# Background weight combinations spread over batches 1 to 3 and stored from SyncE, and low halves of w_out formed by GpSimd, in a fused Nystrom attention and MLP kernel

## The chip, the cores and the metric

The kernel runs on one core of a Trainium2 chip. The metric is the time of one execution on the device in microseconds. Before the change it is 814.55 us, the median of 3 runs (814.32 to 814.81).

## The reference: what is computed

The input is q, k and v of 4 batches, 8 heads, 576 positions and 64 dimensions. Each head goes through a Nystrom attention with 32 landmarks:

```python
q_lm = q.reshape(B, H, m, S // m, D).mean(axis=3)      # m = 32, S = 576
A, Bm, C = sm(q, k_lm), sm(q_lm, k_lm), sm(q_lm, k)    # softmax of scaled products
Z = Bm.T / (norm1(Bm) * norminf(Bm) + 1e-06)
for _ in range(6):
    Z = 2 * Z - Z @ Bm @ Z
x = A @ Z @ C @ v                                      # 2304 tokens x 512
```

Two feed-forward blocks follow, each with weights of 512 x 2048 and 2048 x 512. The first has a leaky rectifier with a slope per channel, the second a gate:

```python
h = x @ w_in;  x = (max(h, 0) + alpha * min(h, 0)) @ w_out
h = x @ w_in2; out = (h * clip(h + 3, 0, 6) / 6) @ w_out2
```

The four weight matrices arrive as 64-bit floats, and the kernel forms 32-bit ones itself.

## The kernel before, in words

Every value that is multiplied at good precision is kept as two halves: ScalarE casts it to a rounded high half (`hi`), and VectorE subtracts that from the value to get the low half (`lo`). The helper `split` (lines 126 to 130) does both, and a product is then three matmuls (`passes`, line 132).

**Stage 1** is attention and the first feed-forward block. The main loop (line 1100) has 128 items, numbered `n`: 4 batches of 32 items, and in a batch two blocks of tokens by 16 tiles of 128 hidden channels. Item `n` issues the 6 matmuls `h` of its own tile (`first`, line 755) and, two items later, the 12 matmuls `acc` with `w_out` (`second`, line 784). Between them ScalarE and VectorE apply the rectifier and split the result: L774, L775, then L128 and L129 on `gs`. The attention of the next batch runs in pieces between the items, one piece per tick (`tick`, line 1097). In batch 0 the first block multiplies by the unsplit words of `w_out`, and at items 14 to 29 the 16 tiles of `w_out` are split by `w_out_split` (line 702) for all later use.

**The background work** of stage 1 prepares the second feed-forward block, which uses a product scheme of 7 multiplications instead of 8. Its weights are cut into 32 subs (16 of `w_in2`, 16 of `w_out2`), and for each sub `forms2` (line 844) goes through five steps, in five consecutive ticks:

- step 0: ScalarE turns the 64-bit words into two parts (L859, L862)
- step 1: VectorE joins the parts (L865), and GpSimd forms four sums or differences of 128x128 (L852)
- step 2: the first three of the seven forms are split into the tile `fa`, and `fa` is stored to DRAM
- step 3: the other four are split into `fb`
- step 4: `fb` is stored

A new sub begins every third tick (`GAP = 3`, `tick2`, line 891), and at that tick the raw words of the sub after it are also loaded (`land2`). 98 ticks are needed. The loop gives one per item from item 22 on, so that the last falls on item 119; `while ticks[0] < GAP * len(subs) + 2` (line 1153) would make up for missing ones. Work of a tick is held behind the rectifier of items `n - 2` and `n - 3`. The tiles `fa` and `fb` share few buffers (`home2`, line 838): two in turn for the first nine tiles, then three in turn, of which one is a slot of `w_out`'s pool. Tile number 9, which is `fb` of sub 4, and tile number 8, which is `fa` of sub 4, have the same buffer.

**Stage 2** is the second feed-forward block, in three blocks of tokens. Its weights are streamed from DRAM into six buffers `st` (`stream`, line 942), which lie where the pools of stage 1 lay. The first unit needs the first two of them.

**The order.** The instructions of TensorE and SyncE stand in the order of the program text (`manual_schedule`, line 1094). Those of ScalarE, VectorE and GpSimd are ordered by a planner, which simulates times and takes what is ready by priority. Every engine then works its own list in order, and an instruction that waits holds up those behind it. SyncE issues all loads of stage 1, and the loads of `stream` come right behind the last tick in its list.

Of the kernel before, what the change touches and what calls it, by code (L numbers as in the profile page):

```python
# [64 lines left out]
def kernel(  # L65
# [60 lines left out]
    def split(hi, lo, src, rest=nc.vector):  # L126
        return (
            nc.scalar.copy(hi, src),  # L128
            rest.tensor_tensor(out=lo, in0=src, in1=hi.bitcast(F32), op=ALU.subtract),  # L129
        )  # L130
# [571 lines left out]
    def w_out_split():  # L702
        for kk in range(NK):
            wout.append(wa.tile([P, 2, 512], F32R, tag=f"s{(kk + NK) % (NK + 1)}", name=f"wout{kk}"))
            split(wout[kk][:, 0], wout[kk][:, 1], words[kk])
            yield True

    wo_gen, wo_split = Background(w_out_tiles()), Background(w_out_split())
# [135 lines left out]
    def forms2(n_):  # L844

        z, i, j = subs[n_]
        raw = raw2[n_]
        high, low = raw[:, :, :, 1], raw[:, :, :, 0]
        x, y = low.bitcast(F32), high.bitcast(F32)

        def combine(o, p, q_, op):
            nc.gpsimd.tensor_tensor(out=y[:, o], in0=p, in1=q_, op=op)  # L852

        def stored(f, fs):
            to = w1_d[:, i, j, fs] if z == 0 else w2_d[:, fs, i, j]
            nc.gpsimd.dma_start(out=to, in_=f.bitcast(F32))  # L856

        if wide:
            nc.scalar.activation(  # L859
                out=high.bitcast(F32), in_=high.bitcast(F32), func=AF.Prelu, scale=2.0 ** -112, alpha=-(2.0 ** 32)  # L860
            )
            nc.scalar.activation(out=low, in_=low.bitcast(U32), func=AF.Copy, scale=0.9374 * 2.0 ** -29)  # L862
        yield True
        if wide:
            nc.vector.scalar_tensor_tensor(  # L865
                out=low, in0=high, scalar=3, in1=low, op0=ALU.logical_shift_left, op1=ALU.bitwise_or
            )
        if z == 0:
            combine(0, x[:, 1], x[:, 0], ALU.subtract)
            combine(2, x[:, 0], x[:, 3], ALU.add)  # L870
            combine(1, x[:, 3], y[:, 0], ALU.subtract)
            combine(3, x[:, 2], y[:, 1], ALU.subtract)
        else:
            combine(0, x[:, 0], x[:, 1], ALU.subtract)
            combine(1, x[:, 3], x[:, 0], ALU.subtract)
            combine(2, y[:, 1], x[:, 1], ALU.add)
            combine(3, y[:, 2], x[:, 2], ALU.subtract)
        yield True
        fa = home2().tile([P, 3, 2, P], F32R, tag=tags2[-1], name="fa")
        split(fa[:, :, 0], fa[:, :, 1], x[:, 1:4])  # L880
        stored(fa, slice(0, 3))
        yield True
        fb = home2().tile([P, 4, 2, P], F32R, tag=tags2[-1], name="fb")
        split(fb[:, :, 0], fb[:, :, 1], y)
        yield True
        stored(fb, slice(3, 7))
# [207 lines left out]
    with tc.manual_schedule(engines={mybir.EngineType.PE, mybir.EngineType.SP}):  # L1094
        pend = []

        def tick(n):
            bg.step(1)

        for n, (x, kk) in enumerate(items):  # L1100
            b, at_ = divmod(n, per)
            if b == 0 and at_ < NK:
                for i, (gen, upto) in enumerate(((wo_gen, min(at_ + 2, NK)), (w_gen, min(at_ + 11, NK + 5)))):
                    with behind(started if at_ < 3 else steps[at_ - 2] + steps[at_ - 3]):
                        gen.step(max(0, upto - emitted[i]))
                    emitted[i] = max(upto, emitted[i])
                if at_ % 4 == 3 and at_ // 4 + 1 < NC:
                    project(0, at_ // 4 + 1)
            if b == 0 and at_ >= NK - 2:
                upto = min(NK, at_ - NK + 3)  # L1110
                with behind(items[n - 1][0].last):
                    wo_split.step(upto - emitted[2])
                emitted[2] = upto
            if b == 0 and at_ in (NK + 4, NK + 6):
                c = NC // 2 + (at_ - NK - 4) // 2
                nc.gpsimd.dma_start(out=keep[:, c], in_=wins[c])
            if b == 0 and at_ == 6:
                bg.add(pinned(rest[0]))
            if b == 0 and at_ == 8 or b and at_ == 5:
                if b + 1 < B:  # L1120
                    bg.add(rush(attention(b + 1, two, 1), 300))
            if b + 1 < B and at_ in (28, 30):
                if at_ == 28:
                    bg.finish()
                project(b + 1, (at_ - 28) // 2)
                fetch(part(b + 1, 2 + (at_ - 28) // 2))
            if b and at_ in (1, 3):
                project(b, 2 + at_ // 2)
            if b == B - 1 and at_ == 4:
                stx.close()  # L1130
                yp = pool("yp", 1, side="right")
                load_y(0)
                y0 = Background(forms_y(0))
            pend.append((n, x, kk, x.first(kk)))
            if n < 3:
                warm((2, 3, 8)[n])
            tick(n)
            while pend and n >= pend[0][0] + (LOOK + 1 if pend[0][2] == 0 else LOOK):
                _, x0, kk0, gs = pend.pop(0)
                for _ in x0.second(kk0, gs):  # L1140
                    tick(n)
                tick(n)
            if n >= NK + 6:
                with behind(steps[n - 2] + steps[n - 3]):
                    tick2()
                    if b == B - 1 and at_ > 6 and at_ % 3 == 0:
                        y0.step(1)
        while pend:
            _, x0, kk0, gs = pend.pop(0)
            drain(x0.second(kk0, gs))  # L1150
        y0.finish()

        while ticks[0] < GAP * len(subs) + 2:
            tick2()

        sty.close()
        NST, NS = 6, 6
        tp = pool("tp", 1)
        stp = pool("st", NST)
        gp_ = pool("g", 1)  # L1160
        sp_ = pool("s", NS)
        g = gp_.tile([P, NK, TB], F32, name="g")
        shomes = [(sp_, "s") if x == "s" else (rp, x) for x in "r0 f0 s s r1 s s f1 s s r2".split()]
        shomes = [(sp_, "s") if x == "s" else (rp, x) for x in "r0 f0 s s r1 s s f1 s s r2".split()]
        ring, sums = [0], {}
        stream(NST)
        for i in range(NB):
            if i + 1 < NB:
                load_y(i + 1)
            for u in range(NU):  # L1170
                unit1(i, u)
            later = Background(forms_y(i + 1)) if i + 1 < NB else Background()
            for n_ in range(7):
                product2(i, n_)
                later.step(1)
            later.finish()
# [32 lines left out]
```

## Time and profile before

| What | Value |
|---|---|
| median of 3 runs | 814.55 us |
| the profiled execution's own time | 816.88 us |
| span of the profile | 815.1 us |
| TensorE busy | 792.8 us (97%) |
| VectorE busy | 594.5 us (73%) |
| ScalarE busy | 464.7 us (57%) |
| GpSimd busy | 185.6 us (23%) |
| DMA, mean over the span | 234 GB/s |

The profile shows one execution, with times in us from the start of its span. PE is TensorE's matmul, DVE is VectorE, ACT is ScalarE, POOL is GpSimd and SP is SyncE. L134 is line 134 of the kernel. The span runs from about 163 us on in batches 1 to 3, and stage 2 begins at about 454 us. TensorE's granted clock is at its full level in nearly all of the span.

### The profile page before, as it was taken

The page shows a single profiled execution, that of the slowest core. Times are in us where ns is not written, and L with a number is a line of the kernel's source. Part 1 is how long each engine was busy: PE and PEld are TensorE (multiplying, and loading weights), DVE is VectorE, ACT ScalarE, POOL GpSimd, SP SyncE. Part 2 cuts the span into 40 slices and gives each one's busy share as a digit, 9 for nine tenths or more (in the row PEclk, how much of TensorE's full clock was granted, in tenths as well). Part 3 has the DMA queues.
Part 4 walks back from the last instruction along what each step waited for, and adds up shares of the span by engine and source line. Part 5 has one row for each costly group of instructions (what it writes and reads, how often), then busy time and mean ns, then how long its engine had stood idle before and what let it go on. Part 6 is the DMA issues. An engine that isn't in the chain of part 4 may idle for free.

```text
span 815.1 us, 16385 instructions
## 1 busy us (share of the span) xinstructions
PE 792.8 (97%) x6146; PEld 739.4 (91%) x6146; DVE 594.5 (73%) x1215; ACT 464.7 (57%) x998; POOL 185.6 (23%) x275
## 2 busy tenths in 40 slices
PE   9788998999999999999999999999999999999997
PEld 6467787888988999988999999999999999999997
DVE  5778688768876778767795477994676994677962
ACT  4697556657665765666664455752455742555541
POOL 0000003244324433443660232000232000322000
PEclk9999999999999999999999999999999999999999
DMA  8998505587384973559655677777867677666751
GB/s 230 408 413 246 137 27 134 215 234 252 117 252 166 318 241 118 173 181 338 211 170 207 262 297 271 283 269 246 319 225 285 259 288 254 246 265 266 260 224 59
DMA packets 92559, 190.87 MB, mean 234 GB/s; under 512 B 39232, under 2 KB 66368, under 8 KB 85824
## 3 DMA queue, kind: packets, MB, share of 16 engines
q1 hardware_dynamic: 82944, 151.55, 53.4%
q0 software_dynamic: 9536, 38.28, 13.5%
q8 instruction: 48, 0.79, 0.4%
q14 instruction: 31, 0.25, 0.1%
HBM read 146.81 MB, written 42.99 MB: 233 GB/s over the span
## 4 chain that ended last, share of the span: by engine, by line
PE 85%; ACT 4%; DVE 4%; DMA 4%; issue 1%; SPq 1%; DVEq 0%; ACTq 0%
PE acc L134 20%; PE l L134 20%; PE qa L1038 15%; PE h L134 11%; PE qb L1038 7%; PE acc L793 2%; PE wp L683 2%; PE sa L433 2%; PE tp L276 1%; PE sc L347 1%; DMA raw<-in_moe_w_out_dram 1%; PE psr L517 1%; DMA raw<-in_moe_w_in_dram 1%; DMA yr<-y_d 1%; DMA w_d<-fa 1%
## 5 line engine op out<-in xcount | busy, mean ns | idle before, releaser
L134 PE MATMUL acc<-gs,wout 128*128 128x288 f32 (+1 forms) x1344 | 207.4, 300 | 0.0
L134 PEld LDWEIGHTS acc<-gs,wout 128*128 128x128 f32 x1344 | 186.1, 188 | 3.4 <-issue 1.5
L134 PE MATMUL l<-yf,st 128*128 128x384 f32 x1008 | 175.5, 335 | 0.7 <-DVE g L985 0.7
L134 PEld LDWEIGHTS l<-yf,st 128*128 128x128 f32 x1008 | 174.6, 188 | 1.0 <-DVE g L985 1.0
L1038 PE MATMUL qa<-st,s 128*128 128x256 f32 x1008 | 148.4, 283 | 0.0
L1038 PEld LDWEIGHTS qa<-st,s 128*128 128x128 f32 x1008 | 133.2, 192 | 0.0
L134 PE MATMUL h<-a,w 128*128 128x288 f32 (+2 forms) x768 | 129.4, 304 | 2.8 <-DVE gs L775 1.9
L128 ACT CAST s<-g 128x384 fp32r<-128x384 f32 x168 | 84.4, 512 | 80.5 <-PE qb L1038 54.2
L134 PEld LDWEIGHTS h<-a,w 128*128 128x128 f32 x768 | 108.4, 188 | 21.2 <-DVE gs L129 5.1
L129 DVE TENSOR_TENSOR s<-g,s 128x384 fp32r<-128x384 f32 x168 | 89.3, 560 | 20.4 <-ACT s L128 17.6
L852 POOL TENSOR_TENSOR raw<-raw 128x128 f32<-128x128 f32 x128 | 74.3, 592 | 76.0 <-DVE raw L865 41.2
L1038 PE MATMUL qb<-st,s 128*128 128x256 f32 x504 | 87.9, 283 | 0.0
L999 POOL TENSOR_TENSOR p<-p,p 128x384 f32<-128x384 f32 x24 | 26.3, 1095 | 237.9 <-ACT p L994 237.9
L774 ACT ACTIVATE t<-h 128x288 f32<-128x288 f32 (+2 forms) x120 | 49.5, 412 | 51.4 <-PE h L134 50.8
L775 DVE SCALAR_TENSOR_TENSOR t<-t,beta,h 128x288 f32<-128x288 f32 (+1 forms) x112 | 57.5, 513 | 28.2 <-ACT t L774 27.5
L1038 PEld LDWEIGHTS qb<-st,s 128*128 128x128 f32 x504 | 72.6, 192 | 0.0
L129 DVE TENSOR_TENSOR gs<-t,gs 128x288 fp32r<-128x288 f32 (+1 forms) x112 | 56.3, 503 | 18.3 <-ACT gs L128 17.9
L128 ACT CAST gs<-t 128x288 fp32r<-128x288 f32 (+1 forms) x112 | 49.0, 438 | 28.0 <-DVE t L775 26.4
L856 POOL DMA_DIRECT2D w_d<-fb x32 | 21.1, 661 | 77.0 <-DVE fb L129 47.6
L984 ACT ACTIVATE ta<-l,three 128x384 f32<-128x384 f32 x24 | 14.0, 583 | 38.5 <-PE l L134 38.5
L793 PE MATMUL acc<-gs,raw 128*128 128x256 f32 x128 | 31.8, 383 | 0.0
L990 ACT COPY p<-l 128x384 f32<-128x384 f32 x24 | 11.5, 479 | 34.5 <-PE l L134 34.5
(204 smaller groups left out, 1053.9 us busy)
## 6 DMA issues: line engine op xcount, KB each, us to landing
st<-w_d SPq DMA_DIRECT2D x48, 896.0 KB, 6.0
st<-w_d SPq DMA_DIRECT2D x42, 1024.0 KB, 5.5
w_d<-fb POOLq DMA_DIRECT2D x32, 512.0 KB, 4.2
w_d<-fa POOLq DMA_DIRECT2D x32, 384.0 KB, 3.2
raw<-in_moe_w_in_dram SPq DMA_DIRECT2D x16, 512.0 KB, 11.8
raw<-in_moe_w_out_dram SPq DMA_DIRECT2D x16, 512.0 KB, 11.5
raw<-in_moe_w_in_dram SPq DMA_DIRECT2D x64, 128.0 KB, 4.9
raw<-in_moe_w_out_dram SPq DMA_DIRECT2D x64, 128.0 KB, 4.8
```

Of the source, the lines that this page charges most:

```text
L128: nc.scalar.copy(hi, src),
L129: rest.tensor_tensor(out=lo, in0=src, in1=hi.bitcast(F32), op=ALU.subtract),
L134: nc.tensor.matmul(ps, lhsT=lhs(x), rhs=rhs(y), start=first and i == 0, stop=last and i == 2, **kw)
L433: nc.tensor.matmul(o[:, :, j], lhsT=qT[:, j, t * P:t * P + n], rhs=bdk[:, j], start=True, stop=True)
L683: nc.tensor.matmul(ps[g][js], lhsT=bd_t[b][gp, js], rhs=w[gp, j, cols], start=True, stop=True)
L774: nc.scalar.activation(out=t, in_=h, func=AF.Relu, scale=-1.0),
L775: nc.vector.scalar_tensor_tensor(out=gs[:, 0] if plain else t, in0=t, scalar=beta[:, kk:kk + 1], in1=h, op0=ALU.mult, op1=ALU.add),
L793: nc.tensor.matmul(acc, lhsT=words[kk][:, ms], rhs=gs[:, 0], start=at_ == 0, stop=at_ == NK - 1)
L852: nc.gpsimd.tensor_tensor(out=y[:, o], in0=p, in1=q_, op=op)
L856: nc.gpsimd.dma_start(out=to, in_=f.bitcast(F32))
L999: nc.gpsimd.tensor_tensor(out=p7, in0=p7, in1=p5, op=ALU.add)
L1038: nc.tensor.matmul(to[t], lhsT=s[:, y, t * P:(t + 1) * P], rhs=w[:, kp % 4, :, z], start=kp == 0 and m == 0 and t != 1, stop=kp == NU - 1 ...
```

## The change

Three things change. The low halves of `w_out` are formed by GpSimd in two pieces of 256 columns, while ScalarE still casts the high halves. The stores of `fa` and `fb` are issued by SyncE instead of GpSimd, and the store of `fa` moves to the beginning of the next step. The ticks run in every item from batch 1 on (items 32 to 127, 96 ticks), and the two that are left run behind the loop. A repeated line, which assigns the same value twice, is dropped.

```diff
@@ def w_out_split():
-            split(wout[kk][:, 0], wout[kk][:, 1], words[kk])
+            nc.scalar.copy(wout[kk][:, 0], words[kk])
+            for cs in (slice(0, 256), slice(256, 512)):
+                nc.gpsimd.tensor_tensor(
+                    out=wout[kk][:, 1, cs], in0=words[kk][:, cs], in1=wout[kk][:, 0, cs].bitcast(F32), op=ALU.subtract
+                )
             yield True
@@ def stored(f, fs):
-            nc.gpsimd.dma_start(out=to, in_=f.bitcast(F32))
+            nc.sync.dma_start(out=to, in_=f.bitcast(F32))
@@ forms2, step 2 and 3
         split(fa[:, :, 0], fa[:, :, 1], x[:, 1:4])
+        yield True
         stored(fa, slice(0, 3))
-        yield True
         fb = home2().tile([P, 4, 2, P], F32R, tag=tags2[-1], name="fb")
@@ main loop
-            if n >= NK + 6:
+            if b:
                 with behind(steps[n - 2] + steps[n - 3]):
                     tick2()
@@ stage 2
-        shomes = [(sp_, "s") if x == "s" else (rp, x) for x in "r0 f0 s s r1 s s f1 s s r2".split()]
         shomes = [(sp_, "s") if x == "s" else (rp, x) for x in "r0 f0 s s r1 s s f1 s s r2".split()]
```

## Rows read from the trace of the kernel before

**Rows 1.** The page, part 1: busy us, share, instructions.

```profile
PE 792.8 (97%) x6146; PEld 739.4 (91%) x6146; DVE 594.5 (73%) x1215; ACT 464.7 (57%) x998; POOL 185.6 (23%) x275
```

**Rows 2.** Windows: busy us and count by engine, clock, DMA share, GB/s.

```profile
100.00:150.00 50.00, 47.30 (x398) 42.84 (x398) 39.54 (x101) 30.89 (x76) 9.37 (x14) 1.00 0.27 77
150.00:200.00 50.00, 47.84 (x386) 42.47 (x385) 36.12 (x65) 32.38 (x71) 19.90 (x35) 1.00 0.83 262
...
400.00:450.00 50.00, 50.00 (x380) 50.00 (x380) 37.88 (x68) 29.50 (x65) 19.00 (x26) 1.00 0.53 185
```

**Rows 3.** TensorE's timeline, 100 to 200 us: start, us, work, [idle before, releaser].

```profile
133.46 0.69 PE L517 MATMUL psr<-nx 128*128 128x96 f32 x4 [0.81 <-ACT nx L530]
...
139.39 0.66 PE L517 MATMUL psr<-nx 128*128 128x96 f32 x4 [0.82 <-DVE nx L534]
...
142.24 0.34 PE L463 MATMUL atp<-ident,epc 64*128 64x64 f32 x2 [0.89 <-DVE a L129]
...
183.73 0.66 PE L276 MATMUL tp<-ident,rk 128*128 128x128 f32 x4 [1.50 <-ACT kT L277]
...
187.09 0.46 PE L276 MATMUL tp<-ident,rk 64*128 64x64 f32 x4 [0.67 <-ACT kT L277]
```

**Rows 4.** ScalarE's timeline ahead of the first of these gaps.

```profile
131.42 0.66 ACT L128 CAST fb<-raw 128x512 fp32r<-128x512 f32 x1
131.98 0.68 ACT L859 ACTIVATE raw<-raw 128x512 f32<-128x512 f32 x1
132.55 0.66 ACT L862 ACTIVATE raw<-raw 128x512 int32<-128x512 uint32 x1
133.10 0.51 ACT L530 ACTIVATE nx<-psr,cs 128x64 f32<-128x64 f32 x2
```

**Rows 5.** VectorE's timeline ahead of the next two gaps.

```profile
136.03 0.69 DVE L865 SCALAR_TENSOR_TENSOR raw<-raw 128x512 int32<-128x512 int32 x1
...
140.30 0.55 DVE L129 TENSOR_TENSOR fa<-raw,fa 128x384 fp32r<-128x384 f32 x1
```

**Rows 6.** Tile wout: duration ns min/median/max, first and last start.

```profile
L129 DVE TENSOR_TENSOR wout<-raw,wout x16: 673/686/693, 94.0 to 154.0; 128x512 fp32r<-128x512 f32 x16
```

**Rows 7.** Tiles raw and p: subtractions and sums on GpSimd.

```profile
L852 POOL TENSOR_TENSOR raw<-raw x128: 399/518/1320, 123.5 to 425.5; 128x128 f32<-128x128 f32 x128
...
L999 POOL TENSOR_TENSOR p<-p,p x24: 1007/1015/1342, 457.6 to 747.0; 128x384 f32<-128x384 f32 x24
```

**Rows 8.** Tile gs: the low half of an item's result on VectorE.

```profile
L129 DVE TENSOR_TENSOR gs<-t,gs x112: 437/459/823, 104.3 to 450.7; 128x288 fp32r<-128x288 f32 x96, 128x320 fp32r<-128x320 f32 x16
```

**Rows 9.** ScalarE's timeline, 160 to 200 us.

```profile
181.81 0.65 ACT L128 CAST fb<-raw 128x512 fp32r<-128x512 f32 x1 [3.67 <-DMA w_d<-fa]
```

**Rows 10.** SyncE's timeline, 130 to 200 us.

```profile
158.63 5.65 SPq L822 DMA_DIRECT2D raw<-in_moe_w_in_dram  x8
165.83 6.64 SPq L240 DMA_DIRECT2D rq<-in_q_dram  x5
```

**Rows 11.** Tile w_d: the 64 stores, us from issue to landing.

```profile
DMA to landing us min/median/max: 2.6/4.8/10.2
```

**Rows 12.** VectorE's timeline, 415 to 456 us.

```profile
420.01 0.69 DVE L865 SCALAR_TENSOR_TENSOR raw<-raw 128x512 int32<-128x512 int32 x1
...
426.73 0.69 DVE L129 TENSOR_TENSOR fb<-raw,fb 128x512 fp32r<-128x512 f32 x1
...
442.54 0.52 DVE L775 SCALAR_TENSOR_TENSOR t<-t,beta,h 128x288 f32<-128x288 f32 x1 [0.91 <-ACT t L774]
```

**Rows 13.** SyncE's timeline, 425 to 475 us.

```profile
436.46 18.46 SPq L947 DMA_DIRECT2D st<-w_d  x6
```

**Rows 14.** Line 947 from 440 to 443 us: two of these loads.

```profile
L947 SPq DMA_DIRECT2D st<-w_d x2: 422/424/425, 440.0 to 440.5; - x2
...
DMA to landing us min/median/max: 6.2/7.0/7.9
```

**Rows 15.** TensorE's timeline, 425 to 460 us.

```profile
453.71 6.58 PE L134 MATMUL l<-yf,st 128*128 128x384 f32 x37
```

## The prediction

> **What bounds the kernel now.** I read the page's busy times first: TensorE is busy for 792.8 of 815.1 us and no other engine is near it [rows 1]. All that can be had or lost is therefore TensorE's idle time, and the second view, the windows of 50 us, says where that lies. From 400 to 450 us, in batch 3, TensorE is busy all 50 us, and the 380 matmuls at 18 per item give 50 / (380 / 18) = 2.37 us per item, while VectorE has 37.9 us and ScalarE 29.5 us of work. From 100 to 150 us (batch 0) TensorE misses 2.7 us, and from 150 to 200 us 2.2 us [rows 2]. So the third view is TensorE's timeline there, which names five gaps. Three lie in batch 0: 0.81, 0.82 and 0.89 us, all at matmuls of the next batch's attention. Two lie in batch 1: 1.50 and 0.67 us at the transposes of k [rows 3]. The last view is what ScalarE, VectorE and SyncE did ahead of each gap, and around the passage to stage 2, since the change pushes work against that passage.
>
> **Batch 0: what is removed.** The change takes ten ticks out of items 22 to 31. Ahead of the first gap ScalarE worked off a cast of fb and two steps of raw, 0.57 + 0.57 + 0.55 = 1.68 us by the starts from 131.42 to 133.10, and only then the scaling of nx for which TensorE waited [rows 4]. All of the 1.68 us goes, which is more than the gap of 0.81 us. Ahead of the second and the third gap VectorE did a join of raw (0.69 us) and the low half of fa (0.55 us) [rows 5], besides low halves of wout, 16 of 0.69 us in all [rows 6], 11 us that go to GpSimd. I count all three gaps as gone: 0.81 + 0.82 + 0.89 = 2.5 us. Bounds: 2.5 us gained, or nothing if contention (below) holds the chain up as long; I take -2.5, since what goes is longer than each gap.
>
> **GpSimd's new work.** The trace has no 128x256 subtraction on GpSimd. From below it is a 128x128 one, 0.52 us, from above a 128x384 one, 1.02 us [rows 7]; I take the middle, an estimate of 0.77 us. Two per tile make 1.5 us, 16 tiles 25 us, at one tile per item, and an item of batch 0 is no shorter than 2.37 us. GpSimd has 9.4 us of work from 100 to 150 us [rows 2], most of it the sums and stores that leave. So it keeps up, and TensorE uses a tile of wout some items after its split: cost nothing, from cover of several items; without the cover a step would wait for the next cast of wout on ScalarE, under 1.5 us each.
> Its price lies on VectorE. The low half of gs takes 0.46 us in the median and 0.82 us at most, where a GpSimd sum runs beside it [rows 8]: up to 0.36 us for such an operation. With one such meeting per tile that is 16 x 0.36 = 6 us against the 11 us taken off, so VectorE is still relieved. The Trainium skill (SBUF — State Buffer, SBUF: two separate sides) states the harder rule that speaks against this part: a VectorE operation with two SBUF inputs and a GpSimd operation that reads SBUF exclude each other for a whole instruction. By that rule VectorE could lose the 25 us that GpSimd works, more than the 11 us it saves; the worst row shows half an instruction lost, so I give it a small chance as a rival.
>
> **Batch 1: a gap that is moved.** The cast of fb of sub 4 waited 3.67 us on ScalarE for the store of fa, which has the same buffer, to land [rows 9], and the copies of the transposes behind it came late: the gaps of 1.50 and 0.67 us. The buffers' order is kept, so this wait comes ten items later, when the next attention is past its transposes, with the store on SyncE's queue. A store landed in 2.6 to 10.2 us, 4.8 in the median [rows 11]. TensorE works two items ahead, 4.7 us; the four operations on an item's result take some 2 us of that (two of them 0.52 and 0.46 us [rows 8, 12]), so a result may be about 2.7 us late before TensorE runs dry. A landing of 2.6 us leaves no gap: 2.2 us gained. One of 4.8 us leaves 4.8 - 2.7 = 2.1 us: nothing gained. I take the middle, -1.0; a landing of 10.2 us would lose 5 us, and is put to the far end of the range.
>
> **Batch 1: the first sub.** Before, the words of sub 0 were loaded long before their tick. Now their loads stand behind the last fetch in SyncE's list, where the row of 158.63 us stands today: 8 issues in 5.65 us, so sub 0's four end near 161.5 us, and with about 6 us to land, as the loads of [rows 14], they are there near 167 us, while ScalarE may want them from 161 us on [rows 10]. Bounds: nothing, or 5.5 us of waiting less the 2.7 us, 2.8 us; I take +0.3, near the lower end, since the planner expects a load's delay as well. The load of q (issued from 165.83 us) now stands behind the stores of sub 0, which wait for VectorE, and slips by about four items, 9 us. It ended its issues at 172.5 us and is used by transposes behind those of 187 us [rows 3, 10]: hidden, with a few us of cover left, each us beyond it a us lost.
>
> **SyncE's queue in the steady part.** 64 stores add 64 issues of about 0.4 to 0.7 us to SyncE (by the loads of [rows 10, 14]), about 1 us of every 7.1 us that a sub takes. Behind a waiting store stand the next raw loads. They had to wait for the same split already, as it frees their buffer: 0, with 0 to +1 us as bounds. GpSimd is freed of its issues; nobody waits for it there.
>
> **The passage to stage 2: what is added.** The list of SyncE ends stage 1 with the stores of fa and fb of sub 31, then come the loads of st. Before, fb's tick fell on item 118 and its low half began at 426.73 us [rows 12]; the first load of st went out at 436.46 us, two others at 440.0 and 440.5 us [rows 13, 14], all landed well ahead of stage 2's first matmul at 453.71 us [rows 15]. Now the ticks of sub 31 lie ten items later, 23.7 us, and the loads are behind the store of fb. When is fb split? Its join waits for the rectifier of item 124, which ends at 442.54 + 0.52 = 443.1 us. Four sums on GpSimd of 0.52 us, the cast and the subtraction of 0.69 us each follow: 443.1 + 0.7 + 2.1 + 0.7 + 0.7 = 447.3 us at the earliest. In the trace the way from the join's start to the end of fb is 427.4 - 420.0 = 7.4 us [rows 12], which gives 450.5 us. I take the middle, D = 449 us. The wait and issue of the store take 0.5 us and the issue of the first load 0.4 us. The load issued next lands 6.2 us after its issue when another is just ahead of it [rows 14]. The store's own half megabyte is in front: 0 to 1.2 us, since a load of st, 896 KB by the code, adds 0.5 + 7.9 - 6.2 = 2.2 us to the one before it [rows 14] and fb has 512 KB; I take 0.6. The second buffer is then full at 449 + 0.9 + 6.2 + 0.6 = 456.7 us. TensorE wants it half a microsecond after 453.7 us, at 454.2: it waits 2.5 us. Bounds: D = 447.3 without the store ahead gives 0.2 us, D = 450.5 with 1.2 us gives 4.6 us. Batch 3 itself costs nothing: it ran without gaps with ticks and VectorE has 12 us free in 50 [rows 2].
>
> **The sum.** -2.5 - 1.0 + 0.3 + 0 + 2.5 = -0.7 us on the profiled execution's 816.88 us (its span is 815.1 us, the rest lies around it). That execution is 2.3 us above the median of the runs; the difference is carried over to the median: 814.55 - 0.7 = 813.9 us. What a measurement can tell from no change is 0.2%, 1.6 us: faster is below 812.9, slower above 816.2.
>
> **Rivals.**
> *The loads of st come late.* If the planner puts the last cast of fb behind the copies of the last sums (after 453 us), D is about 455 us, TensorE waits 456.7 + 6 - 454.2 = 8.5 us, and the time is near 820; behind the rectifier of item 127 (D = 451.5) it is 816.4. It decides from D = 451.3 on. For it: those two ticks have no item to hold them and stand last in the text. Against: their inputs are ready before, and ScalarE has 40% free. Between the two 818, chance 0.20.
> *The loads come in time.* D near 447.5 and the batch 1 gaps gone entirely: -2.5 - 2.2 + 0.3 + 0.4 = -4.0, 810.6; chance 0.20. For it: the ten items of batch 3 are lightly loaded. Against: fa's own store must land first as well.
> *The gaps only move.* The wait for the store of fa of sub 4 leaves its 2.2 us (no gain) and the late words of sub 0 cost 2.8 us: -2.5 + 0 + 2.8 + 2.5 = +2.8, 817.3 at worst; with half of the words' price 816; chance 0.10. For it: the two waits stand in the code. Against: the planner sees both.
> *Contention in batch 0.* VectorE loses as much as it saves, the 2.5 us stay: 813.9 + 2.5 = 816.4; chance 0.08. For it: the worst meeting of [rows 8]; against: the median of the same row. The Trainium skill's rule above would do this.
> *The forecast,* 813.9, has 0.42; alone it spans 812.0 to 816.0.
>
> **How the numbers follow.** Faster by over 0.2%: all of the second rival, 0.20, and 0.13 of the forecast: 0.33. Slower: 0.18 of the first, 0.04 of the third, 0.04 of the fourth and 0.01 of the forecast: 0.27. Within: 0.40. The range is 810.6 to 818: below it lies little, above it the far end of the first rival.
>
> **What would show it.** Right: no gap at psr and atp from 130 to 143 us; the gaps of 183 and 187 us gone or at a wait for fb near item 47; the first load of st at 449 to 451 us behind the store of fb, and a TensorE gap of 2 to 3 us ahead of the first l, released by a load. Wrong: gaps in batches 2 and 3, VectorE operations lengthened all through batch 0, no gap ahead of stage 2, or one above 5 us.

## The result, and the profile after

The changed kernel is slower: 824.42 us in the median of 4 runs (823.34 to 828.21), against 814.68 us (4 runs, 814.32 to 815.7) for the kernel before. The ratio is 1.0126, with a 95% interval of 1.0092 to 1.016. The forecast was 813.9 us, in a range up to 818. The profiled execution of the changed kernel took 823.34 us, with a span of 821.3 us, 6.2 us longer than the 815.1 us of before.

Part 1 of the page of the changed kernel, which answers to [rows 1] (busy us, share, instructions):

```profile
PE 794.5 (97%) x6146; PEld 739.1 (90%) x6146; DVE 588.5 (72%) x1199; ACT 465.4 (57%) x998; POOL 172.7 (21%) x243
```

TensorE's work is the same 6146 matmuls; VectorE has 16 operations and 6 us less, GpSimd 32 instructions less (64 stores gone, 32 subtractions come). TensorE's idle time grows from 22.3 us to 26.8 (span less busy time): most of the 6.2 us went there, and the windows say where. Windows of the changed kernel, columns as in [rows 2]:

```profile
100.00:150.00 50.00, 49.65 (x422) 44.30 (x421) 31.94 (x83) 26.63 (x70) 21.62 (x28) 1.00 0.15 36
150.00:200.00 50.00, 49.69 (x391) 44.11 (x390) 33.69 (x60) 31.30 (x69) 12.36 (x22) 1.00 0.74 229
200.00:250.00 50.00, 47.94 (x441) 44.73 (x439) 38.67 (x104) 30.04 (x80) 13.35 (x22) 1.00 0.60 181
300.00:350.00 50.00, 47.67 (x439) 42.75 (x437) 39.88 (x103) 29.34 (x78) 12.94 (x22) 1.00 0.51 169
400.00:450.00 50.00, 49.12 (x370) 48.66 (x369) 43.01 (x75) 36.02 (x77) 23.01 (x31) 1.00 0.61 195
450.00:500.00 50.00, 47.53 (x286) 46.88 (x285) 31.24 (x55) 24.26 (x45) 12.29 (x13) 1.00 0.87 336
```

From 100 to 200 us TensorE now misses 0.7 us, where it missed 4.9 [rows 2]: the part that the change was to mend is mended. But 200 to 250, 300 to 350 and 450 to 500 us miss 2.1 to 2.5 us each (before: 0.9, 0.5 and 0), and batch 3 (400 to 450 us), which ran without a gap, misses 0.9. The gaps of over 0.7 us by name, from TensorE's timeline of the changed kernel (columns as in [rows 3]):

```profile
203.12 0.74 PE L347 MATMUL sc<-kT,qlm 64*32 64x320 f32 x8 [1.53 <-ACT epc L373]
...
274.62 1.68 PE L683 MATMUL wp<-win,bd 64*32 64x512 f32 x16 [1.15 <-DVE w L129]
327.51 0.30 PE L480 MATMUL ctp<-ident,epc 128*64 128x128 f32 x1 [0.97 <-ACT ct L477]
344.07 0.34 PE L463 MATMUL atp<-ident,epc 64*128 64x64 f32 x2 [1.17 <-DVE a L129]
...
426.67 1.72 PE L134 MATMUL acc<-gs,wout 128*128 128x288 f32 x11 [0.78 <-DVE gs L129]
459.72 16.42 PE L134 MATMUL l<-yf,st 128*128 128x384 f32 x93 [1.41 <-DMA st<-w_d]
477.19 4.08 PE L134 MATMUL l<-yf,st 128*128 128x384 f32 x22 [1.05 <-DVE h L1013]
```

The gaps of [rows 3] are gone; these are new. None is long, and busy time hides how they add up, so a second measure helps. Both kernels have the same 6146 matmuls in the same order, so each can be set against itself: its start in the changed kernel less its start before. The delay is -2.33 us at the atp of 142.24 us [rows 3], -3.82 at the tp of 187.09, -1.63 at the wp that follows at 276 us, +0.06 at the ctp of 327 us, +1.25 at atp (343), +3.75 at acc (423), +3.86 at the first l [rows 15], and +6.2 at the end. So 3.8 us were won by 187 us, as forecast or better; 7.6 us were lost between 187 and 423 us, where nothing was expected; and the passage to stage 2, from its first l on, cost 2.35 us.

In the same way the start is read for every experiment below; "lost in batches 1 to 3" is the delay at 423 us less that at 187 us, "passage" what comes after 423 us. They are from one profiled execution each, and the ratios from all runs, 4 to 12 of each changed kernel against 4, 17 or 21 of the kernel before that were taken with them. The last tick's item follows from the item of the first.

The column "at 187 us" has to be read with care. At 120 us, before any edit has moved TensorE, the delay is already 0.9 to 1.3 us in e1, e4, e5, e6, e9 and e11 and 0.5 us in e7, and at most 0.3 us in the others: in these executions TensorE's granted clock was low for a while near 41 us (e1 had 0.66 from 40 to 50 us, the kernel before 1.00). From 120 to 187 us alone, e1 gains 2.5 us, e5 2.5, e11 1.5, and the changed kernel 4.0. What is lost behind 187 us isn't touched by this; the delay at the end is.

| Kernel | first tick | stores | ratio [95%] | at 187 us | lost in batches 1 to 3 | passage | end |
|---|---|---|---|---|---|---|---|
| changed | 32 | SyncE | 1.0126 [1.0092, 1.016] | -3.8 | 7.6 | 2.5 | +6.2 |
| e1_low | 22 | GpSimd | 0.9985 [0.9976, 0.9994] | -1.3 | -0.3 | -0.8 | -2.4 |
| e2_store | 22 | SyncE | 1.0098 [1.0083, 1.0114] | +3.6 | 3.5 | 0.5 | +7.6 |
| e3_shift | 32 | GpSimd | 1.0117 [1.0103, 1.0131] | -4.3 | 5.6 | 6.9 | +8.2 |
| e4_shift_low | 32 | GpSimd | 1.0138 [1.012, 1.0156] | -2.7 | 4.6 | 8.9 | +10.7 |
| e5_start31 | 31 | GpSimd | 1.0029 [1.0018, 1.004] | -1.4 | 0.2 | 2.1 | +0.9 |
| e6_start23 | 23 | GpSimd | 1.0039 [1.0026, 1.0053] | -2.6 | 5.3 | -0.5 | +2.1 |
| e7_end | 32 | GpSimd | 1.0109 [1.0091, 1.0126] | -3.9 | 4.5 | 7.5 | +8.1 |
| e8_store_early | 22 | SyncE, early | 1.0042 [1.0026, 1.0058] | -1.3 | 3.2 | -0.6 | +1.3 |
| e9_low28 | 28 | GpSimd | 1.0004 [0.9995, 1.0014] | -1.6 | 1.3 | -0.6 | -0.9 |
| e10_low25 | 25 | GpSimd | 0.9986 [0.9976, 0.9996] | -3.7 | 0.1 | 0.5 | -3.1 |
| e11_full31 | 31 | SyncE | 1.0079 [1.0066, 1.0092] | -0.6 | 4.4 | 1.6 | +5.4 |
| e12_early28 | 28 | SyncE, early | 1.0048 [1.0034, 1.0061] | -2.7 | 6.0 | -0.5 | +2.8 |

The low halves on GpSimd are in e1, e4, e9, e10, e11, e12 and in the changed kernel.

### The profile page after: what moved, and what is told of

It reads as the page before. It is cut to its first block, busy times and chain, and to the rows that moved or that the text cites. A ratio compares the mean times of both kernels' runs of the same rounds, so it can differ in the third digit from the quotient of the medians.

```text
span 821.3 us, 16439 instructions
## 1 busy us (share of the span) xinstructions
PE 794.5 (97%) x6146; PEld 739.1 (90%) x6146; DVE 588.5 (72%) x1199; ACT 465.4 (57%) x998; POOL 172.7 (21%) x243
## 4 chain that ended last, share of the span: by engine, by line
PE 75%; DMA 9%; DVE 6%; ACT 5%; issue 2%; SPq 2%; POOL 1%; DVEq 0%; ACTq 0%; POOLq 0%
PE l L134 20%; PE qa L1042 15%; PE acc L134 14%; PE h L134 8%; PE qb L1042 7%; DMA raw<-in_moe_w_out_dram 4%; PE acc L797 2%; DMA st<-w_d 2%; DMA raw<-in_moe_w_in_dram 2%; DMA w_d<-fa 2%; PE sa L433 2%; PE wp L683 2%; PE tp L276 1%; SPq L826 1%; PE sc L347 1%
## 5 line engine op out<-in xcount | busy, mean ns | idle before, releaser
L856 POOL TENSOR_TENSOR raw<-raw 128x128 f32<-128x128 f32 x128 | 79.8, 639 | 189.8 <-DVE raw L869 126.1
L129 DVE TENSOR_TENSOR gs<-t,gs 128x288 fp32r<-128x288 f32 (+1 forms) x112 | 60.9, 544 | 22.5 <-ACT gs L128 22.1
L707 POOL TENSOR_TENSOR wout<-raw,wout 128x256 fp32r<-128x256 f32 x32 | 24.6, 789 | 41.9 <-ACT wout L705 28.9
## 6 DMA issues: line engine op xcount, KB each, us to landing
raw<-in_moe_w_in_dram SPq DMA_DIRECT2D x16, 512.0 KB, 11.2
```

The source lines that it names most:

```text
L707: nc.gpsimd.tensor_tensor(out=wout[kk][:, 1, cs], in0=words[kk][:, cs], in1=wout[kk][:, 0, cs].bitcast(F32), op=ALU.subtract)
```

## Experiments

### Each part by itself: e1 to e4

**The low halves alone.**

```diff
@@ w_out_split
-            split(wout[kk][:, 0], wout[kk][:, 1], words[kk])
+            nc.scalar.copy(wout[kk][:, 0], words[kk])
+            for cs in (slice(0, 256), slice(256, 512)):
+                nc.gpsimd.tensor_tensor(
+                    out=wout[kk][:, 1, cs], in0=words[kk][:, cs], in1=wout[kk][:, 0, cs].bitcast(F32), op=ALU.subtract
+                )
```

> Only the low halves of w_out go to GpSimd; ticks from item 22 and stores by GpSimd as before. Queue theory (the 7.6 us lost in batches 1 to 3 come from the stores standing in SyncE's list) and position theory (they come from the ten items' shift, which sets the background work against other pieces of attention and fills the end of batch 3) both expect no loss in batches 1 to 3 here: 812 to 815 us, with up to 2 us of the three batch 0 gaps regained. The contention rival expects 815 to 818.

Measured: 814.36 us, ratio 0.9985 [0.9976, 0.9994], a gain of 0.15%, in the range that both theories gave. The new subtractions on GpSimd in the changed kernel, then VectorE's low halves of gs from 93 to 153 us, beside which they run, in the kernel before and in e1:

```profile
L707 POOL TENSOR_TENSOR wout<-raw,wout x32: 737/747/1011, 94.2 to 152.2; 128x256 fp32r<-128x256 f32 x32
L129 DVE TENSOR_TENSOR gs<-t,gs x12: 473/484/810, 104.3 to 150.5; 128x320 fp32r<-128x320 f32 x12
L129 DVE TENSOR_TENSOR gs<-t,gs x12: 483/690/1028, 105.3 to 149.7; 128x320 fp32r<-128x320 f32 x12
```

The median of all 112 in the span of the changed kernel is 459 ns, as before [rows 8], but most of them lie where no subtraction runs. In the stretch with subtractions the median rises from 484 to 690 ns (618 in the changed kernel, 1061 at most): about 0.2 us for nearly every one of 12, some 2.5 us against the 11 us taken off VectorE. TensorE loses nothing by it. This part isn't where the time went.

**The stores alone**, with the first tick at item 22 as before. As in the change, the store of fa also moves a step later.

```diff
@@ stored
-            nc.gpsimd.dma_start(out=to, in_=f.bitcast(F32))
+            nc.sync.dma_start(out=to, in_=f.bitcast(F32))
@@ forms2, step 2 and 3
-        stored(fa, slice(0, 3))
         yield True
+        stored(fa, slice(0, 3))
```

> Only the stores move to SyncE (with the store of fa one step later); ticks from item 22. Queue theory: gaps in batches 1 to 3 as in the changed kernel, 818 to 822 us, and raw loads and stores issued later than before. Position theory: 814 to 816 us, with the gaps of 183 and 187 us still there.

Measured: 823.15 us, 1.0098 [1.0083, 1.0114], a little above the range of the queue theory. The stores by themselves cost nearly as much as the whole change. Of the first 3.6 us, 2.0 are lost at an acc and a wp of batch 1 (165 and 172 us), which wait 0.64 and 0.45 us for VectorE, and the rest at the transposes of k; TensorE, ScalarE and the windows of e2 there:

```profile
186.49 1.11 PE L276 MATMUL tp<-ident,rk 128*128 128x128 f32 x4 [2.27 <-ACT kT L277]
```

```profile
185.31 0.65 ACT L128 CAST fb<-raw 128x512 fp32r<-128x512 f32 x1 [2.82 <-DMA w_d<-fa]
```

```profile
180.00:185.00 5.00, 4.22 (x34) 3.98 (x32) 2.28 (x5) 1.40 (x4) 2.42 (x4) 1.00 0.68 239
185.00:190.00 5.00, 3.51 (x16) 3.50 (x17) 2.92 (x4) 4.15 (x9) 0.00 (x0) 0.66 0.26 105
```

It is the wait of [rows 9], for the store of fa of sub 4 to land, ended 3.5 us later in the span. Here that store went out 3.5 us after its split, where it was 1.1 us before; SyncE's list and the step by which it is later both enter. Behind the wait stands the copy kT, and TensorE's gap is 2.27 us where it was 1.50 [rows 3]. After the gap the granted clock is 0.66 in the next 5 us, a mean of time at the full level (2.4 GHz) and at the lower one (1.2): the gap is paid for again in slow matmuls.

**The later ticks alone.**

```diff
@@ main loop
-            if n >= NK + 6:
+            if b:
```

> Only the ticks move to items 32 to 127; stores by GpSimd. Queue theory: 810 to 814 us, since batch 0 and the two gaps in batch 1 are regained (4 us) and only the passage to stage 2 costs 1 to 3 us. Position theory: 818 to 822 us, with gaps in batches 1 to 3 at the same kinds of places as in the changed kernel.

Measured: 824.84 us, 1.0117 [1.0103, 1.0131], above the ranges of both theories. It wins 4.3 us by 187 us, loses 5.6 in batches 1 to 3 and 6.9 at the passage. The new gaps of batch 2 are those of the changed kernel, at ctp and atp, though SyncE issues no store here. At the passage, e3's TensorE, then SyncE, then windows:

```profile
457.73 0.80 PE L134 MATMUL l<-yf,st 128*128 128x384 f32 x3 [2.03 <-DMA st<-w_d]
460.51 4.85 PE L134 MATMUL l<-yf,st 128*128 128x384 f32 x14 [1.98 <-DMA st<-w_d]
```

```profile
452.83 3.71 SPq L947 DMA_DIRECT2D st<-w_d  x6
```

```profile
455.00:460.00 5.00, 1.51 (x9) 0.95 (x7) 0.87 (x2) 0.40 (x1) 1.43 (x2) 0.90 0.99 374
460.00:465.00 5.00, 4.49 (x14) 4.49 (x15) 0.00 (x0) 0.96 (x2) 0.00 (x0) 0.50 1.02 411
```

The loads of st go out at 452.83 us instead of 436 to 440 us [rows 13, 14], and TensorE waits 2.03 and 1.98 us for them; then the granted clock is 0.50, the lower level, for 5 us in which only 14 matmuls run. So the passage is late by the shift of the ticks alone, whoever issues the stores.

**The low halves and the later ticks**, both edits above, without the stores.

```diff
@@ w_out_split
-            split(wout[kk][:, 0], wout[kk][:, 1], words[kk])
+            nc.scalar.copy(wout[kk][:, 0], words[kk])
...
@@ main loop
-            if n >= NK + 6:
+            if b:
```

> Everything of the change but the queue: ticks in items 32 to 127 and low halves on GpSimd, stores by GpSimd. Queue theory: 810 to 814 us. Position theory: 819 to 824 us, near the changed kernel's 824.

Measured: 826.82 us, 1.0138 [1.012, 1.0156]: above both ranges and no better than e3, with the same two waits at l (1.98 and 2.03 us). The costs of e2 and e3, 1.0% and 1.2%, aren't additive, since the whole change comes to 1.26%. The changed kernel is e4 with the stores on SyncE, and isn't slower than e4: it loses 3.0 us more in batches 1 to 3 and 6.4 us less at the passage. What is lost ahead of the passage makes TensorE come later to loads that land no sooner, so it waits less for them.

### Why the later ticks lose time in batches 2 and 3: e5 and e6

A sub begins every third tick and the attention's pieces keep their items. A first tick at item 32 instead of 22 moves the background by ten items, which three doesn't divide: other steps now stand ahead of the same piece of attention. ScalarE ahead of the ctp of 327 us, in the changed kernel, and the like stretch of the kernel before:

```profile
324.88 0.41 ACT L778 ACTIVATE t<-h 128x288 f32<-128x288 f32 x1 [0.74 <-PE h L134]
325.19 0.67 ACT L128 CAST fb<-raw 128x512 fp32r<-128x512 f32 x1
325.75 0.69 ACT L863 ACTIVATE raw<-raw 128x512 f32<-128x512 f32 x1
326.32 0.66 ACT L866 ACTIVATE raw<-raw 128x512 int32<-128x512 uint32 x1
326.87 1.07 ACT L477 COPY ct<-ctp 128x512 f32<-128x512 f32 x2
```

```profile
323.37 0.65 ACT L128 CAST fb<-raw 128x512 fp32r<-128x512 f32 x1
323.92 0.68 ACT L859 ACTIVATE raw<-raw 128x512 f32<-128x512 f32 x1
324.49 0.67 ACT L862 ACTIVATE raw<-raw 128x512 int32<-128x512 uint32 x1
...
325.96 0.41 ACT L774 ACTIVATE t<-h 128x288 f32<-128x288 f32 x1 [0.17 <-PE h L134]
326.37 1.08 ACT L477 COPY ct<-ctp 128x512 f32<-128x512 f32 x2
```

Step 3 of a sub (the cast of fb) and step 0 of the next (two operations on raw) fall on one tick, 1.68 us of ScalarE by the starts. Before, this tick came an item ahead of the copy of ct; now it stands between a rectifier and the copy, and TensorE waits 0.97 us. If that is the cause, a start at 31 (nine items later) must lose nothing in these batches, and a start at 23 (one later) as much as 32.

```diff
@@ main loop, e5
-            if n >= NK + 6:
+            if n >= NK + 15:
```

> Ticks from item 31 on, stores and low halves as before: one item earlier than the shift alone, so that in batches 1 and 2 the three-item rhythm of the background work stands against the pieces of attention as it stood before (22 and 31 leave the same remainder by 3). Rhythm theory (the shift alone lost its 6 us in batches 1 to 3 because the casts and unpackings fell just ahead of the copies of ctp and atp in batch 2): no gap at ctp and atp in batch 2, delay against before at 380 us of -4 to -2 us; the passage to stage 2 still costs 1 to 6 us; 814 to 820 us. Lateness theory (it is the later and denser place, whatever the rhythm): gaps as with the shift alone, delay at 380 us of -1.5 to 0 us, 822 to 825 us.

```diff
@@ main loop, e6
-            if n >= NK + 6:
+            if n >= NK + 7:
```

> Ticks from item 23 on, stores and low halves as before: one item later than before, ten ticks still in batch 0, the rhythm that of the shift by ten items. Rhythm theory: gaps at ctp and atp in batch 2 (near 325 and 342 us) as with the shift alone, some 2 to 4 us lost there; 816 to 820 us. Lateness theory: no such gaps, 814 to 816 us.

Measured: e5 818.05 us, 1.0029 [1.0018, 1.004]; e6 819.32 us, 1.0039 [1.0026, 1.0053]. Both times and the gaps came as the rhythm theory has them, but e5's delay at 380 us didn't: -1.15 us, where -4 to -2 was expected (the 1.1 us that stand at 120 us included). TensorE of e5 from 300 to 350 us (only the lines with a wait for another engine), then of e6:

```profile
331.20 0.90 PE L492 MATMUL pu<-rv,ct 128*32 128x64 f32 x40 [0.35 <-ACT nx L497]
...
340.21 0.66 PE L463 MATMUL atp<-ident,epc 128*128 128x128 f32 x4 [0.19 <-DVE a L129]
```

```profile
326.06 0.30 PE L480 MATMUL ctp<-ident,epc 128*64 128x128 f32 x1 [0.97 <-ACT ct L477]
326.55 0.30 PE L480 MATMUL ctp<-ident,epc 128*64 128x128 f32 x1 [0.19 <-ACT ct L477]
...
342.69 0.34 PE L463 MATMUL atp<-ident,epc 64*128 64x64 f32 x2 [1.17 <-DVE a L129]
```

One item of shift brings the gaps of the changed kernel, 0.97 and 1.17 us at the same matmuls, and 5.3 us of loss in batches 1 to 3; nine items bring 0.2 us. Half of the 5.3 us lies at these two matmuls; of the rest, 2.3 us lie in batch 3, at an h (389 us of before) and around 420 us, in e3 as in e6 and not in e5. What stands ahead of those is open. Over all kernels whose stores stay on GpSimd, first ticks at 22, 25, 28 and 31 lose -0.3 to 1.3 us there, and 23 and 32 lose 4.5 to 5.6. The remainder by three decides, not the amount of the shift. What e5 still loses is the passage: 1.31 us of wait at l, 2.1 us in all, nearly as much as the 2.5 us that it gains from 120 to 187 us.

### The passage: e7

If only the shared buffer of the last fa and fb holds the loads of st back, these tiles kept out of the slot of w_out's pool should free them. The ticks are those of e3.

```diff
@@ home2
-        spare = i > 8 and i % 3 == 2
-        tags2.append(f"s{NK - 1}" if spare else f"f{i % 3 % 2 if i > 8 else i % 2}")
+        ring3 = 8 < i < 60
+        spare = ring3 and i % 3 == 2
+        tags2.append(f"s{NK - 1}" if spare else f"f{i % 3 % 2 if ring3 else i % 2}")
```

> The shift alone (ticks in items 32 to 127, stores by GpSimd), with the last two subs' tiles fa and fb kept out of the slot of w_out's pool, so that the first load of stage 2 doesn't wait for the last store of fa. Passage theory (with the shift alone, that store's landing at 452.7 us set the first load's issue at 452.8 us, TensorE stood 2.0 and 2.0 us and then ran at the lower clock level from 460 to 465 us): the loads go out near 441 us, no gap and no lower clock at the start of stage 2, 6 us less than the shift alone, 816 to 819 us. Rival (the stage's start is late for another reason, such as the loads' own time): 822 to 825 us.

Measured: 824.9 us, 1.0109 [1.0091, 1.0126]; the expectation failed. The loads did go out early, but the stores of the last subs then came late. SyncE, ScalarE and TensorE of e7:

```profile
442.10 1.91 SPq L948 DMA_DIRECT2D st<-w_d  x4
```

```profile
450.45 0.53 ACT L128 CAST fa<-raw 128x384 fp32r<-128x384 f32 x1 [4.29 <-DMA w_d<-fa]
...
453.88 0.65 ACT L128 CAST fb<-raw 128x512 fp32r<-128x512 f32 x1 [2.57 <-DMA w_d<-fb]
```

```profile
451.37 0.40 PE L134 MATMUL acc<-gs,wout 128*128 128x288 f32 x1 [1.40 <-ACT gs L128]
...
456.20 5.33 PE L134 MATMUL acc<-gs,wout 128*128 128x288 f32 x24 [2.48 <-ACT gs L128]
```

With two buffers instead of three ScalarE waits 4.29 and 2.57 us for stores that landed 8.1 and 9.7 us after their issue, beside the loads, and the casts of gs stand behind it. The wait moved and stayed as long. What the passage needs is background work that ends earlier, as it does in all kernels with first ticks up to 28 (passage -0.8 to +0.5 us).

### The queue of SyncE: e8, and e11 beside e5

SyncE's list in the changed kernel around 230 us:

```profile
214.61 0.33 SPq L860 DMA_DIRECT2D w_d<-fa  x1
228.10 4.27 SPq L240 DMA_DIRECT2D rk<-in_k_dram  x5
232.47 0.57 SPq L860 DMA_DIRECT2D w_d<-fb  x1
233.14 3.68 SPq L826 DMA_DIRECT2D raw<-in_moe_w_in_dram  x4
236.92 0.38 SPq L860 DMA_DIRECT2D w_d<-fa  x1
```

The store of fb at 232.47 us was ready at 220.2: VectorE split that tile from 219.57 us on. It stood behind the load of k, and raw loads stood behind it in turn. What the load of k waited for, from SyncE's waits of that stretch (us in total, times, longest):

```profile
SPq L240 <- PE pu L492: 13.1, 1, 13.1
```

A load that feeds the attention waits 13.1 us for a matmul, and a finished store with it. Over the 64 stores, from the end of VectorE's split to the issue, the changed kernel takes over 4 us for 16 of them and 12.2 us at most; before, it was one of 64. In e8 each store is issued in the step of its own split, which puts it ahead of the next fetch more often; the first tick is at item 22. The edit against e2:

```diff
@@ forms2, step 2 to 4, against e2
+        stored(fa, slice(0, 3))
         yield True
-        stored(fa, slice(0, 3))
         fb = home2().tile([P, 4, 2, P], F32R, tag=tags2[-1], name="fb")
         split(fb[:, :, 0], fb[:, :, 1], y)
-        yield True
         stored(fb, slice(3, 7))
+        yield True
```

> Stores by SyncE with ticks from item 22 (as in the run with the stores alone, 823 us), but each store stands in the step of its split, one step earlier for both. Place theory (a store is held up because it stands in SyncE's list behind loads that wait for TensorE, two to three items later than VectorE does the split): fewer stores late by over 4 us than 18 of 64, and 817 to 821 us. Rival (the loads are held up by stores that wait for VectorE): raw loads go out later than with the stores alone, 823 us or more.

Measured: 820.1 us, 1.0042 [1.0026, 1.0058]; 9 stores are over 4 us late, where e2 has 18, and the cost falls from 0.98% to 0.42%. The same transfers by the same engine, each one step earlier in SyncE's list, cost less than half as much. Against the kernel before, e8 keeps the store of fa in its old step and has that of fb a step earlier, so its 0.42% doesn't come from later steps. The rival's sign, raw loads that go out later, is there as well (see e12 below), but the time fell all the same.

The whole change but with the first tick at 31, so that the remainder by three is that of before:

```diff
@@ main loop, against the changed kernel
-            if b:
+            if n >= NK + 15:
```

> The whole change, but ticks from item 31 instead of 32, which gives batches 1 and 2 the old rhythm. If rhythm, place in SyncE's list and passage are three separate causes, only the first goes: 817 to 821 us against the 824 of the whole change, with no gaps at ctp and atp in batch 2. If the queue alone made the losses with the shift: 823 to 826 us.

Measured: 822.15 us, 1.0079 [1.0066, 1.0092], between the two ranges. The gap at ctp is gone and that at atp is 0.19 us, yet 4.4 us are lost in batches 1 to 3, where e5, with the stores on GpSimd and without the low halves, lost 0.2. By the ratios the remainder by three would be worth 0.5% of the changed kernel's 1.26% (1.26 to 0.79), but the two intervals touch, and the profiles show less: at 423 us both kernels are 3.8 us late, since e11 gains less by 187 us, and the end differs by 0.8 us. So both causes are there, but how the 1.26% divides between them is not shown.

### What is left of the gain: e9, e10, e12

All three have the low halves on GpSimd. e9 and e10 leave the stores there too, e12 has them on SyncE as e8 has.

```diff
@@ main loop, e9
-            if n >= NK + 6:
+            if n >= NK + 12:
```

> Low halves on GpSimd, ticks from item 28 on (same remainder by 3 as 22), stores by GpSimd. Rhythm theory, with the passage costing nothing when the last tick falls on item 125: the gaps of batch 0 and those of 183 and 187 us go and nothing comes in their place but a wait for the first words, 810 to 813 us, ahead of the kernel before by 0.2 to 0.5%. Rival (any delay of the background work is paid in batches 1 to 3): 815 to 819 us.

```diff
@@ main loop, e10
-            if n >= NK + 6:
+            if n >= NK + 9:
```

> The same with ticks from item 25 on: one period earlier, so the last tick falls on item 122, but five to seven ticks stay in batch 0 ahead of its gaps. Rhythm theory: 811 to 814 us. Rival: 815 to 818 us.

```diff
@@ main loop, e12, against the changed kernel
-            if b:
+            if n >= NK + 12:
```

> The whole change with all three causes eased: ticks from item 28 (old rhythm, last tick on item 125) and each store by SyncE in the step of its split. If the three causes are all there is: 812 to 817 us, near the kernel before, with what is left of SyncE's waits. If something else in the change costs time: 820 us or more.

Measured: e9 815.84 us, 1.0004 [0.9995, 1.0014]; e10 814.31, 0.9986 [0.9976, 0.9996]; e12 819.4, 1.0048 [1.0034, 1.0061]. The expectations were too hopeful: e9 lies in the range of its rival, e12 between its two ranges and e10 just above its own. e9 has new gaps in batch 1 (1.19 us at 165 us, 1.08 at 205 us) which eat what the shift wins, and e12 differs from e9 only in the stores and is 0.44% above it: even issued early, they cost that much on SyncE. The transfers themselves aren't slower: the stores land 3.3 us after their issue in the median in e12, and 3.7 in e9. In e12's profile 6 are over 4 us late.

The two profiles show where e12 loses against e9. TensorE near 243 us in e9, then in e12, and ScalarE of e12 in batch 3:

```profile
243.51 0.89 PE L506 MATMUL psr<-nx 128*128 128x192 f32 x4 [0.46 <-DVE nx L534]
243.47 1.15 PE L506 MATMUL psr<-nx 128*128 128x192 f32 x4 [1.82 <-DVE nx L534]
```

```profile
392.94 0.67 ACT L863 ACTIVATE raw<-raw 128x512 f32<-128x512 f32 x1 [2.83 <-DMA raw<-in_moe_w_out_dram]
```

At the first place e12 comes 1.4 us ahead of e9 and loses that lead in its longer gap; behind it the granted clock is 0.66 from 243 to 248 us, and at 276 us e12 is 1.5 us behind e9. From 380 to 423 us e12 loses another 2.1 us and e9 0.1; there ScalarE waits 2.83 us for words of the next sub, and e9 has no such wait near 393 us. So loads stand behind stores too: from the last of a sub's four loads to ScalarE's first use of the words e9 has 10.6 us in the median and e12 7.3 (the kernel before 11.2, e2 9.8, e8 7.6). How much of the queue's cost comes from late stores and how much from late loads is not separated.

e10 is as good as e1: both are 0.14 to 0.15% faster than before, the only versions that beat both kernels, and the later first tick adds nothing to the low halves that these runs can tell.

## Why the prediction was wrong, point by point

**The step that failed** is "SyncE's queue in the steady part", put at 0 with bounds of 0 to +1 us, and with it the sentence "Batch 3 itself costs nothing" and the silence on batch 2. Measured: 7.6 us lost between 187 and 423 us. The prediction had named gaps in batches 2 and 3 as a sign that it was wrong. Two mechanisms make the loss.

*The queue.* The prediction counted 64 issues of about half a microsecond and asked who stands behind a store: only raw loads, which wait for the same split. It didn't ask what a store stands behind. [Rows 10] show the load of q on SyncE's list, and the prediction itself noted that it would wait behind stores; the reverse, a store behind loads that wait for TensorE, was left out. SyncE works its list in the program's order; behind a load that waits 13.1 us, a finished tile keeps its buffer, and ScalarE waits for the buffer with attention's copies behind it (2.82 us in e2, 2.45 in the changed kernel at 196 us). Nor was it nothing for the raw loads that stand behind a store: they go out 3.3 us closer to their use in e12 than in e9. e12 against e9 (+0.44%) shows the price with the stores as the only difference, and e8 against e2 (0.42% instead of 0.98%) that it follows from the place in the list. e2 against before has the later step of fa in it, and e11 against e5 (+0.5) the low halves. Beside e4, the changed kernel loses 3.0 us more in batches 1 to 3.

*The remainder by three.* The prediction moved ten items' ticks and priced what left batch 0, not what the shift does to the tick that falls ahead of each later piece of attention. Whether a window has free time said nothing of it: ScalarE's busy share in the 300 to 350 us window is 29.34 of 50 us, under 60%, and the gap comes from 1.68 us in the wrong place. e5 and e6 show it, with nothing else changed.

**Batch 0** was right: -2.5 us forecast; from 120 us to the last of the three gaps the delay goes from 0.14 to -2.33 us. The later ticks alone do as much: in e3 it goes from 0.29 to -2.25. e1, with the low halves alone, keeps the first gap (0.81 us, as [rows 3]), loses the second and has 0.33 us at the third: the last two hung on VectorE, as [rows 5] had it, and the first on ScalarE's ticks. Either edit alone is enough for the second.

**GpSimd's new work** was right: estimate 0.77 us, measured 0.75 in the median, and no wait of TensorE for w_out. The price on VectorE was put at up to 0.36 us each, 6 us; it was about 0.2 us for most low halves of gs in that stretch, some 2.5 us. The rival of contention, by which the gain in batch 0 stays away, is refuted for this kernel by e1. The Trainium skill (SBUF — State Buffer, SBUF: two separate sides) states an exclusion for whole instructions; low halves of gs lengthened from 484 to 690 ns in the median beside subtractions of 747 ns agree with meetings, and don't show whether the lock holds for the whole instruction.

**Batch 1** was right in the sum or better, -0.7 forecast and -1.5 measured (from -2.33 to -3.82 us), though both terms were larger than forecast. The transposes gain 2.5 us, not 1.0. ScalarE waited 2.73 us for the words of sub 0, and TensorE lost 1.0 us at the wp of 169 us, not 0.3. The wait of [rows 9] that was to come "ten items later" didn't: the store of fa of sub 4 landed 2.3 us after its issue, and the cast of fb at 208.9 us had nothing to wait for. [Rows 11] had been misread there: they mix the loads of stage 2 with the stores, which alone landed in 2.6 to 7.5 us, 3.7 in the median. Another store delayed a cast instead, that of fa of sub 2. It went out 2.6 us after its split, took 7.0 us to land, and the cast of fa of sub 3 waited 2.45 us for it at 196 us, ahead of the gap of 1.53 us at sc. That gap is part of the 7.6 us; no rival had it.

**The passage** was right in its path and, in part by luck, in size: forecast +2.5, measured 1.41 and 1.05 us of gaps, +2.35 in the end. SyncE and VectorE there, in the changed kernel:

```profile
449.98 0.36 SPq L860 DMA_DIRECT2D w_d<-fa  x1
451.66 0.36 SPq L860 DMA_DIRECT2D w_d<-fb  x1
452.58 6.00 SPq L951 DMA_DIRECT2D st<-w_d  x6
```

```profile
450.94 0.69 DVE L129 TENSOR_TENSOR fb<-raw,fb 128x512 fp32r<-128x512 f32 x1 [0.41 <-ACT fb L128]
```

fb is split at 451.6 us; less the 3.86 us by which TensorE is late there, that is D = 447.8, forecast 449. The first load stands right behind the store, as forecast, though the last 0.4 us of its wait were for the store of fa to land. Two things were not: only 1.41 us of the wait is for the load, the other 1.05 us being for VectorE (L1013); and the same shift without the stores (e3, e4) costs 6.9 and 8.9 us. In e3 TensorE is only 1.8 us late when it comes to the first l, and the first load goes out at 452.83 us, no earlier than here. So it waits longer, 4.0 us in all, and the granted clock falls (0.50 from 460 to 465 us).

**The rivals.** None of them is what happened. Late loads of st needed D from 451.3 us on, and it was 447.8; the gaps at the transposes went, so they didn't only move; and contention took nothing from the gain in batch 0. The chance given to slower was 0.27, and none of it stood for gaps in batches 2 and 3.

## What to carry to other kernels

Before a DMA is moved to another engine's list, ask what it will stand behind there, not only what will stand behind it: a list that works in order gives it the wait of every entry ahead. Before periodic work is shifted against other work, write down which step meets which for the old and the new offset; a shift by whole periods keeps the old meetings, and any other makes new ones. And where two edits each cost 1% alone, they needn't cost 2% together: here a loss early in the kernel shortened a wait behind it. Comparing the same instruction's start through all versions shows where.

## What the hardware showed that was not expected

TensorE's granted clock fell after short stalls: to 0.66 over 5 us behind one gap of 2.27 us (e2), to 0.50 behind two of about 2 us (e3), and to 0.66 behind one of 1.82 us (e12), while the changed kernel's gaps of 1.53 us at 203 us and 1.41 us at 460 us left it at 1.00.

The engine that issues a DMA mattered far beyond the issue's own time. The Trainium skill (DMA: Bandwidth & Descriptors, Issuing engines are not separate DMA queues) states that transfers share the same DMA engines whoever starts them, and that starting them from several engines saves only the time of initiating. On the first the runs agree: a store lands about as fast from either (3.7 us in the median in e9, 3.3 in e12). On the second the measurement differs: of the 64 stores GpSimd issued one over 4 us after its split, and SyncE 18, up to 12.7 us late (e2), and 6 where they are issued early (e12), with 0.44% of the time as the price.

Left open: whether stores on SyncE could be free if they were put ahead of the attention's loads in its list. That order was not tried. Nor was any kernel run that moves the stores to SyncE and leaves both in the steps that they had before.
